# Rounding turns in PSUM with TensorE products in place of a VectorE instruction, in a four-layer spectral kernel

## The chip, the cores and the metric

The kernel runs as one launch on one core of a Trainium2 chip. The metric is the device time of that launch in microseconds (us), as the median of its runs. A core has five engines that run side by side and wait for one another through semaphores: TensorE (PE, matrix products into PSUM), VectorE (DVE), ScalarE (ACT), GpSimd (POOL) and SyncE (SP, which here issues the transfers). Each of them takes its own instructions in order.

## The reference, cut to what matters

An input x of 2048 x 512 passes through four layers, each added to x after a layer norm: A, B, A, B. A is a product with fixed weights in the two-dimensional Fourier domain. B is a convolution along the 2048 positions, one filter K per channel, made through a Fourier transform of twice the length. The filter comes from 128 complex modes per channel, and its making is what the change touches:

```python
dt = jnp.exp(log_dt)
A = -jnp.exp(log_A_real) + 1j * A_imag
C = (C_real + 1j * C_imag) * dt[:, None]
P = jnp.exp((A * dt[:, None])[:, :, None] * pos[None, None, :])
K = 2.0 * jnp.einsum("dn,dnl->dl", C, P).real
```

So for each channel d, position l and mode n the kernel needs a magnitude exp(...) and the sine and cosine of an angle. The angle is counted in turns (one turn is 2 pi). Whole turns change nothing, and the sine instruction is given an angle between minus half a turn and half a turn, so whole turns are taken off first.

## The kernel before, in words

**Stages.** The work of 2048 positions is split as 16 x 128. The first layer A has three parts: `spread` (layer norm and the first Fourier step), `middle` (line 566: `forward`, `weigh`, `back`) and `end` (`fold`, `rows_back`). Layer B works by blocks of 128 channels: `kernel_freq` (line 928) transforms the filter, `forward_norm` and `forward_b` (line 640) the input, `layer_b` (line 970) weighs the two (`weigh`) and transforms back (`back`). Then come the second A and the second B, with the filter's transform kept in memory (kf) from the first time.

**The filter from modes** is `kernel_time` (line 815). Its first inputs come from `kernel_parts` (line 726), which makes, from the raw mode parameters, five rows of values per channel and mode, and splits each into three bf16 parts, which go through memory (parts) into the tile `th` (96 partitions: two halves of three parts of 16 channels). There are 32 units i of 16 channels, and for each unit:

- `grow(i)` (line 834): two products of `th` with constant tiles RM and RP (slices of the constant tile `kb`) into a PSUM tile `pk` and two exponentials by ScalarE into `mag` (line 832 is the helper that records ScalarE's instructions); GpSimd makes a third magnitude (lines 847 and 848).
- for j = 0 and 1, `bend(i, j)` (line 855): four TensorE products of `th` with 256 columns of KQ and KP, also slices of `kb`, put 2 x 256 angles in turns into a PSUM tile `pk` of 128 x 512. VectorE (line 864) adds and takes off a large constant, MAGIC = 1.5 x 2^23, at which float32 has no digits behind the point, and so leaves the rounded turns in the bf16 tile `kw`. TensorE then takes them off the angles in place, as a product of `kw` with `ni`, a negative identity, accumulated onto the same PSUM tile.
- `sine(i, j)` and `cosine(i, j)` (ScalarE, line 832): the absolute angle into the tile `kf`, the sine in place in `pk`, the cosine from `kf` into `qp`.
- `terms(i, j)` (VectorE, lines 886 and 888): four products of sines and cosines with magnitudes into `qp`.
- `total(i, j)`: sixteen TensorE instructions (line 899) sum over the modes into the PSUM tile `pv`; ScalarE copies them to `stage` (line 907), and SyncE writes them to memory (kt).

That makes 64 bends. The helper `halves` (line 330) issues every product as two, on 64 of the 128 weight columns each; the two write to different halves of the PSUM tile's partitions. A float32 product appears in the profile as two instructions, a bf16 product as one.

**What sets the order.** The filter's steps K are not a stage of their own: they are interleaved with layer A's middle and end, and with the first B, by the fractions FILL (lines 1146 to 1217). The final order of each engine's instructions is written out by hand: TURNS (line 1230) holds, for tensor, vector, scalar, gpsimd and sync, a permutation of that engine's instructions as the program issued them, and `take_turns` (line 1500) imposes it. ROOMS (line 1464) gives, for tiles with several buffers, which buffer each use gets. WARM (line 1452) gives places at which `ps` puts products with the tile `warm` ahead of real work: fill, whose results nobody reads. Each of its entries is a number of calls of `halves` with 128 float32 columns, hence four instructions a call. The sum of its entries is 231.

**Buffers.** PSUM has eight banks of 128 x 512 float32. In this part of the kernel three are for `pk`, one for `pv` (PK and PV) and four for layer A or B. The context manager `phase` opens a pool of tiles; a tile got its place there when it was first asked for.

Of the kernel before, what the change touches and what calls it, by code (L numbers as in the profile page):

```python
# [10 lines left out]
F32 = mybir.dt.float32  # L11
# [27 lines left out]
WT = 4  # L39
# [52 lines left out]
def constants():  # L92
# [111 lines left out]
    out["ni"] = -np.eye(128)  # L204
    out["kb"] = kb.reshape(96, 2560)
# [47 lines left out]
class Net:  # L253
# [553 lines left out]
    def kernel_constants(self):  # L807

        BF = mybir.dt.bfloat16
        self.kb = self.sb("kb", [2560], dt=BF, rows=96)  # L810
        self.ni = self.sb("ni", [128], dt=BF)
        self.nc.gpsimd.dma_start(self.kb, self.cst["kb"])
        self.nc.gpsimd.dma_start(self.ni, self.cst["ni"])

    def kernel_time(self, parts, kt, units, group):
# [6 lines left out]
        KQ, RM, RN, KP, RP = (KB[:, k:k + 512] for k in range(0, 2560, 512))  # L822
# [8 lines left out]
        def ordered(*a, **k):  # L831
            nc.scalar.activation(*a, **k)  # L832
# [22 lines left out]
        def bend(i, j):  # L855
# [8 lines left out]
            nc.vector.tensor_scalar(whole, p, MAGIC, -MAGIC, op0=ALU.add, op1=ALU.add)  # L864
            self.halves(p, self.ni, whole, start=False, stop=True, skip_group_check=True)
            live[i, j] = p, mag

        def sine(i, j):
# [3 lines left out]
            ordered(p, p, ACT.Sin, scale=-TAU)  # L872
# [251 lines left out]
def net_kernel(ctx, tc, x, w, ends, kin, log_dt, d_skip, out, **cst):  # L1124
# [19 lines left out]
    with ExitStack() as outer:  # L1144
        with ExitStack() as early:
            early.enter_context(net.phase("pk", P, pk=(2048, PK), pv=(2048, PV)))
            with net.phase("p", P, p1=(2048, 8 - PK - PV), p2="p1", p3="p1"), \
                    net.phase("a", x=(32768, 1), ta=(8192, 1), ca=(6912, 1), u=(16384, 2), w=(2056, WA), wt=(2056, WT),
                              wv="w", junk="w"):
                A = net.layer_a(w, src=xv, dst=hd)  # L1150
                early.enter_context(net.phase("k0", side="right", kb=(5120, 1), ni=(256, 1), th=(1536, TH)))
                net.kernel_constants()
                with net.phase("v", val=(10240, 1), hp=(HP, 2)):
# [5 lines left out]
                    early.enter_context(net.phase("k", side="right", kw=(1024, 2), mag=(6144, MAG),  # L1159
# [10 lines left out]
            outer.enter_context(net.phase("b", t2=(8192, 1), u=(16384, 2), kk=(2048, 8), ta="t2", wt="w", wb="w", xw="w"))  # L1170
# [61 lines left out]
0-17 23-24 18-19 25-28 20-21 32-39 22 29-31 40-65 67-70 76-79 66 80-81 71-72 82-83 73-75 85-88 94-95 84 89-92  # L1232
103-106 93 96-97 112-113 107-108 98-101 109-110 102 114-115 111 116-119 121-124 120 125-126 130-131 127-128
132-133 129 134-161 172-179 163-168 180-181 169-171 182-193 162 194-211 218-219 234-235 212-217 220-221 236-241
222-225 242-249 256-259 226-231 260 264-266 250 267 251 261 232 268-272 252 262 273 253 263 233 274-279 298-307
280-281 254 312 282 286 255 313 287 314 288 315 289 283-285 308-311 316-321 290-291 322-331 338-339 292-295
340-342 346-349 343-345 296-297 350-351 332-335 366-371 358-365 336-337 374-387 414-417 372-373 402-413 418-423
464-465 424-427 388-393 448-451 466-467 452-455 476-483 512-513 456-461 514-515 394-397 516-517 398-401 462-463
428-431 518-519 432-433 520-523 434 436-437 435 438-439 352-357 548-551 554-557 524-525 468-475 552-553 440-441
484-487 558 492-494 504 495 559 505-507 488-491 442-447 496-497 526-533 498-499 508-511 500-503 534-543 560-561  # L1240
544-547 562-564 568 580 569 581 570 582 571 583 565-567 606-609 572-573 586-593 574-577 584 594 578 612 579 595
613 585 610 596-597 611 614-617 620-621 618-619 598-599 626-627 600-601 622-623 628 634-635 629-630 636-637
631-633 654-657 602-605 638-639 660-667 624-625 640-643 658 668-670 688 671 689 659 690-691 646-651 672-673
652-653 644-645 674-677 694-701 678 702-704 692 705 693 679 738-741 706-711 680-685 752-757 712 760 758 761 759
713 742-743 686 762-763 687 764-771 798-800 808-809 801-807 810-811 772-773 812 834-837 813-815 714-721 774-775
784-785 816-819 838-839 786-787 722-729 788-791 840-843 792-795 730-737 844-845 796-797 820-823 826-831 854-857
878 900-902 832-833 744-749 858-863 750-751 910 824-825 846-849 776-777 850-851 778-783 942 903 852-853 904-906
879-880 886-887 864-875 888 881-884 907-908 943-944 894-896 889-890 945 876-877 946-948 885 909 897 911-912
891-893 926-936 949 898 937-938 913-914 939 915-917 899 970-973 940-941 918-925 974-975 962-969 950-961 976-983
986-987 1032-1033 988-989 984-985 990-997 1006-1009 1034-1035 1010-1015 1054-1055 998-1003 1036-1039 1004-1005  # L1250
1056-1057 1076-1077 1040-1043 1016-1023 1044-1045 1066-1067 1024-1031 1078-1081 1068-1075 1046-1051 1082-1083
1052-1053 1084-1089 1094-1097 1092-1093 1090-1091 1058-1063 1110-1113 1100-1101 1132-1135 1098-1099 1102-1109
1116-1123 1130-1131 1114-1115 1136-1137 1064-1065 1138-1139 1164-1169 1140-1143 1146-1147 1124-1127 1148-1149
1144-1145 1150-1151 1128-1129 1152-1153 1184-1187 1154-1155 1202-1205 1156-1163 1170-1171 1188-1189 1172-1181
1206-1207 1182-1183 1190-1193 1296-1299 1208-1209 1194-1201 1314-1329 1268-1275 1330-1331 1300-1313 1332-1333
1210 1212 1214 1217 1211 1213 1219 1221 1215 1223 1225 1216 1218 1227 1220 1222 1224 1226 1388-1395 1228-1230
1232 1231 1233-1234 1236 1235 1237-1238 1240 1239 1241-1242 1244 1243 1245 1470-1477 1454-1461 1246-1252 1254
1253 1255 1257 1256 1258-1259 1261 1260 1262-1263 1265 1264 1267 1266 1478-1483 1494-1497 1462-1469 1276-1280
1282 1281 1283 1285 1284 1286-1287 1289 1288 1290-1291 1293 1292 1295 1294 1484-1487 1506-1509 1488-1489
1510-1517 1490-1493 1518-1521 1530-1533 1498-1505 1536-1539 1548-1553 1534-1535 1372 1370-1371 1373 1375 1374  # L1260
1376 1378 1380 1377 1379 1382 1381 1383-1384 1386 1385 1387 1540-1541 1554-1555 1334-1351 1580 1352-1353
1581-1583 1626-1633 1354-1357 1584-1585 1594-1597 1680-1685 1658-1659 1686-1687 1660-1661 1358-1360 1598-1599
1396-1397 1399 1398 1401 1403 1400 1402 1405 1407 1404 1406 1409 1411 1408 1410 1361-1363 1688-1691 1662-1663
1364-1369 1692-1693 1412-1425 1427 1429 1426 1428 1431 1433 1430 1432 1435 1437 1434 1436 1708-1713 1698-1701
# [283 lines left out]
```

## Time and profile before

| | |
|---|---|
| time, median of 3 runs | 717.33 us |
| lowest and highest run | 716.2 and 723.59 us |
| span of the profiled execution, first to last instruction | 713.4 us |
| instructions profiled | 23503 |
| mean granted TensorE clock | 0.973 |
| bytes moved by DMA, mean rate | 81.32 MB, 114 GB/s |
| first and last rounding by VectorE (line 864) | 79.8 and 382.9 us |

The profiled execution's own time is not listed apart from the three runs; its span lies 3.9 us under their median. Times in the profile count from its first instruction. How to read its lines:

- A row of the windows view gives a stretch in us, its length, then for each engine the busy time and, in brackets, the number of instructions; then the granted TensorE clock (1.00 is full speed), the DMA share and GB/s. Where a view is asked for one tile alone, only the instructions that read or write it count, and engines without any are left out.
- A row of the groups gives line, engine, operation, tiles (output<-inputs), shapes and the count; then busy time in us and the mean duration of one in ns; then how long the engine stood idle ahead of these instructions, and what ended it.
- A row of the waits names who waited for whom, the total in us, the number of times and the longest.
- A row of the timeline gives start, length, engine, line, operation, tiles, shape and how many are merged in it. Products are pipelined, so a length contains a latency; the distance between starts tells how long the array is held.

PEld is the loading of weights, which overlaps products.

### The profile page before, as it was taken

Reading aid. Unit: us, or ns where it says so; the run is one execution under the profiler, and the core shown is the slowest. Engines: PE = TensorE matmul, PEld = TensorE weight load, DVE = VectorE, ACT = ScalarE, POOL = GpSimd, SP = SyncE. Lnnn points to the kernel's source line nnn. Section 1 sums busy time; section 2 is a strip of 40 time slices with the busy share of each in tenths; the row PEclk is TensorE's granted clock in tenths of the full one; section 3 lists DMA queues with packets and bytes.
Section 4 is the critical chain, followed back from the end, with each engine's and each line's share of the span. In section 5 each row is a group of like instructions: output and inputs, shape, how many; then the busy total and the mean of one; then the engine's idle time right before and its main releaser. Section 6 shows DMA issues by size and latency. Waiting matters only on the chain. (4 is left out here: it accounts for less than half of the span.)

```text
span 713.4 us, 23503 instructions
## 1 busy us (share of the span) xinstructions
PE 626.0 (88%) x9580; PEld 491.3 (69%) x9580; DVE 601.9 (84%) x1348; ACT 438.2 (61%) x946; POOL 357.3 (50%) x565
## 2 busy tenths in 40 slices
PE   4459989989996999889999997984989899999996
PEld 3237867878674867667858876774877766577876
DVE  4998497998999799969999676869588699799993
ACT  3558999997664796778868524333767427333322
POOL 1533528672852704543196356452056484286870
PEclk9779999999999999999999999997999999999999
DMA  8602611613558350455544689222123103335514
GB/s 282 229 0 89 210 48 47 122 62 43 167 133 245 107 138 32 65 128 94 163 62 136 195 198 246 80 106 75 61 77 89 46 2 104 125 103 149 156 34 111
DMA packets 137355, 81.32 MB, mean 114 GB/s; under 512 B 70976, under 2 KB 116928, under 8 KB 136352
## 3 DMA queue, kind: packets, MB, share of 16 engines
q1 hardware_dynamic: 136992, 79.30, 40.1%
q8 instruction: 76, 1.25, 0.7%
q0 software_dynamic: 256, 0.52, 0.4%
q14 instruction: 31, 0.25, 0.1%
HBM read 54.90 MB, written 25.43 MB: 113 GB/s over the span
## 5 line engine op out<-in xcount | busy, mean ns | idle before, releaser
L1003 POOL TENSOR_TENSOR u<-wb,wb 64x512 f32<-64x512 f32 x90 | 123.2, 1373 | 66.0 <-DVE wb L991 60.9
L336 PE MATMUL p<-z,mb 128*64 128x512 f32 (+2 forms) x480 | 108.0, 517 | 1.7 <-DVE wb L991 1.3
L899 PE MATMUL pv<-qp 128*64 128x128 f32 x1024 | 81.6, 279 | 5.0 <-ACT stage L907 4.2
L991 DVE TENSOR_TENSOR wb<-p,kk 128x512 f32<-128x512 f32 x128 | 81.5, 676 | 4.3 <-POOL u L1003 2.3
L336 PEld LDWEIGHTS p<-mb,u 128*64 128x64 f32 x2048 | 73.1, 138 | 13.1 <-issue 6.7
L336 PE MATMUL p<-mb,u 128*64 128x64 f32 x2048 | 74.3, 223 | 4.4 <-issue 2.0
L663 ACT COPY z<-p 128x512 f32<-128x512 f32 x96 | 52.4, 595 | 41.8 <-PE p L336 31.6
L669 DVE STREAM_TRANSPOSE z<-z 128x512 f32<-128x512 f32 x96 | 59.3, 675 | 19.8 <-ACT z L663 19.7
L899 PEld LDWEIGHTS pv<-qp 128*64 128x64 f32 x1024 | 64.4, 139 | 15.8 <-ACT stage L907 6.9
L1113 POOL TENSOR_SCALAR w<-w,norms 128x128 f32<-128x128 f32 x64 | 34.7, 554 | 67.7 <-DMA w<-h 29.8
L547 POOL TENSOR_TENSOR w<-w,w 64x257 f32<-64x257 f32 x48 | 34.7, 724 | 66.8 <-DVE w L542 45.3
L1015 ACT COPY u<-p 128x512 f32<-128x512 f32 x64 | 35.9, 590 | 48.7 <-PE p L336 45.3
L330 PE MATMUL p<-w,w 128*64 128x256 f32 x256 | 38.2, 438 | 27.8 <-DVE w L463 11.6
L330 PE MATMUL pk<-kb,th 96*64 96x256 bf16 (+1 forms) x384 | 56.5, 312 | 1.5 <-DVE qp L888 1.1
L542 DVE TENSOR_TENSOR w<-wt,p 128x514 f32<-128x514 f32 x64 | 42.7, 688 | 17.1 <-PE p L336 9.6
L864 DVE TENSOR_SCALAR kw<-pk 128x512 bf16<-128x512 f32 x64 | 42.9, 680 | 16.5 <-PE pk L330 16.1
L330 PE MATMUL p<-warm 128*64 128x128 f32 x612 | 49.2, 284 | 3.2 <-DVE half L1139 1.1
L336 PE MATMUL p<-t,w 64*64 64x128 f32 x1024 | 42.1, 280 | 10.2 <-DMA w<-kt 3.5
L336 PEld LDWEIGHTS p<-z,mb 128*64 128x64 f32 x480 | 39.7, 137 | 16.1 <-issue 7.9
L330 PEld LDWEIGHTS p<-w,w 128*64 128x64 f32 x256 | 24.7, 156 | 36.3 <-DVE w L463 12.7
L336 PE MATMUL p<-w,ca 128*64 128x257 f32 x256 | 45.0, 385 | 4.1 <-ACT w L526 1.5
L832 ACT ACTIVATE kf<-pk 128x512 f32<-128x512 f32 x64 | 38.8, 606 | 15.4 <-PE pk L330 13.8
(179 smaller groups left out, 1617.1 us busy)
## 6 DMA issues: line engine op xcount, KB each, us to landing
wt<-in_w SPq DMA_DIRECT2D x32, 257.0 KB, 2.7
kf<-kk SPq DMA_DIRECT2D x32, 256.0 KB, 3.3
kk<-kf SPq DMA_DIRECT2D x32, 256.0 KB, 2.7
u<-in_x SPq DMA_DIRECT2D x16, 256.0 KB, 6.8
hr<-in_x SPq DMA_DIRECT2D x16, 256.0 KB, 3.9
kt<-stage SPq DMA_DIRECT2D x32, 128.0 KB, 5.2
h<-hr SPq DMA_DIRECT2D x16, 256.0 KB, 3.0
w<-kt SPq DMA_DIRECT2D x32, 128.0 KB, 3.1
```

The costliest lines, as they stand in the source:

```text
L330: self.nc.tensor.matmul(out[64 * r:64 * r + 64], weights[:, 64 * r:64 * r + 64], data, **k)
L336: last = self.nc.tensor.matmul(out, weights, data, start=not more, stop=True, skip_group_check=True).ins
L542: nc.vector.tensor_mul(m[pl], W, px[:, None, :].to_broadcast([128, 2, 257]))
L547: e[0].tensor_sub(Y[0:64, v], m[0][hs, 0], m[1][hs, 1])
L663: nc.scalar.copy(tiles["z"][:, :, :, b, m:m + 2].rearrange("p u j m r -> p (u j) (m r)"), ps[b].rearrange("p u j m r -> p (u j) (m r)"))
L669: nc.vector.transpose(tiles["zt"][:, u:u + 8].rearrange("p u j d -> p (u j d)"), tiles["z"][:, u:u + 8].rearrange("p u j b m r -> p (u j b ...
L832: nc.scalar.activation(*a, **k)
L864: nc.vector.tensor_scalar(whole, p, MAGIC, -MAGIC, op0=ALU.add, op1=ALU.add)
L899: nc.tensor.matmul(p[64 * t:64 * t + 64, g], QP[:, c, 2, d:d + 2].rearrange("p s a -> p (s a)"), QP[:, c, 0:2, d:d + 2].rearrange("p k s b ...
L991: nc.vector.tensor_mul(split(m[c, pl], "du", [32, 16]), by_channel(p), split(k[c], "du", [32, 16]))
L1003: self.added = e[0].tensor_sub(y[0:64], v[0, 0], v[1, 1]), e[1].tensor_add(y[64:128], v[0, 1], v[1, 0])
L1015: nc.scalar.copy(V[:, :, j, :, d:d + 8].rearrange("p n q d -> p q n d"), p.rearrange("p (q n) d -> p q n d", q=2))
```

## The change

`bend` no longer uses VectorE. TensorE adds MAGIC to the angles in PSUM, as a product whose weights are a row of ones (`ni`, now 256 columns: a first row of 1 in the first half, of -1 in the second, zero elsewhere) and whose data is a tile `big` full of MAGIC; a second product takes MAGIC off. What stays in PSUM is the rounded turns. Then the angles themselves are taken off by four more products of `th` with LQ and LP, which are KQ and KP with the sign turned. What is left is the rounded turns less the angle, where it was the angle less the rounded turns, so the sine's scale changes its sign. The tile `kw` goes, `kb` grows from 2560 to 3584 columns, and a GpSimd memset fills `big`.

Beside it, `phase` reserves a place for every buffer when it opens, in the order in which its tags are written, and two of the phases list their tags in another order. TURNS is rewritten for all five engines, and ROOMS for nearly all tiles. WARM has other places, and the sum of its entries is 145.

```diff
@@ constants
-    out["ni"] = -np.eye(128)
-    out["kb"] = kb.reshape(96, 2560)
+    first = np.zeros((128, 2, 128))
+    first[0, 0], first[0, 1] = 1, -1
+    out["ni"] = first.reshape(128, 256)
+    out["kb"] = np.concatenate([kb, -kb[:, :, :512], -kb[:, :, 1536:2048]], 2).reshape(96, 3584)
@@ phase
             for tag, v in tags.items():
                 self.tags[tag] = self.tags[v] if isinstance(v, str) else (pool, name, tag, *v)
+            for tag, v in tags.items():
+                if not isinstance(v, str):
+                    for k in range(v[1]):
+                        room = f"{tag}{k}" if v[1] > 1 else tag
+                        pool.tile([128, v[0] // 4], F32, tag=room, bufs=1, name=f"{name}_{room}")
             yield
@@ kernel_constants
-        self.kb = self.sb("kb", [2560], dt=BF, rows=96)
-        self.ni = self.sb("ni", [128], dt=BF)
+        self.kb = self.sb("kb", [3584], dt=BF, rows=96)
+        self.ni = self.sb("ni", [256], dt=BF)
+        self.big = self.sb("big", [512], dt=BF)
+        self.nc.gpsimd.memset(self.big, MAGIC)
@@ kernel_time
-        KQ, RM, RN, KP, RP = (KB[:, k:k + 512] for k in range(0, 2560, 512))
+        KQ, RM, RN, KP, RP, LQ, LP = (KB[:, k:k + 512] for k in range(0, 3584, 512))
@@ bend
-            whole = self.sb("kw", [512], dt=BF)
             p = self.ps("pk", [2, 256])
-            self.halves(p[:, 0], th[:, h, 0], KQ[:, e], start=True, stop=False, skip_group_check=True)
-            self.halves(p[:, 1], th[:, h, 1], KP[:, e], start=False, stop=False, skip_group_check=True)
+            a, b = th[:, h, 0], th[:, h, 1]
+            self.halves(p[:, 0], a, KQ[:, e], start=True, stop=False)
+            self.halves(p[:, 1], b, KP[:, e], start=False, stop=False)
+            p0, p1 = p[:, 0], p[:, 1]
             p = p.rearrange("p k d -> p (k d)")
-            nc.vector.tensor_scalar(whole, p, MAGIC, -MAGIC, op0=ALU.add, op1=ALU.add)
-            self.halves(p, self.ni, whole, start=False, stop=True, skip_group_check=True)
+            self.halves(p, self.ni[:, 0:128], self.big, start=False, stop=False)
+            self.halves(p, self.ni[:, 128:256], self.big, start=False, stop=False)
+            self.halves(p0, a, LQ[:, e], start=False, stop=False)
+            self.halves(p1, b, LP[:, e], start=False, stop=True)
             live[i, j] = p, mag
@@ sine
-            ordered(p, p, ACT.Sin, scale=-TAU)
+            ordered(p, p, ACT.Sin, scale=TAU)
@@ net_kernel
-                    net.phase("a", x=(32768, 1), ta=(8192, 1), ca=(6912, 1), u=(16384, 2), w=(2056, WA), wt=(2056, WT),
+                    net.phase("a", x=(32768, 1), u=(16384, 2), ta=(8192, 1), w=(2056, WA), ca=(6912, 1), wt=(2056, WT),
...
-                early.enter_context(net.phase("k0", side="right", kb=(5120, 1), ni=(256, 1), th=(1536, TH)))
+                early.enter_context(net.phase("k0", side="right", kb=(7168, 1), ni=(512, 1), big=(1024, 1), th=(1536, TH)))
...
-                    early.enter_context(net.phase("k", side="right", kw=(1024, 2), mag=(6144, MAG),
+                    early.enter_context(net.phase("k", side="right", mag=(6144, MAG), 
...
-            outer.enter_context(net.phase("b", t2=(8192, 1), u=(16384, 2), kk=(2048, 8), ta="t2", wt="w", wb="w", xw="w"))
+            outer.enter_context(net.phase("b", kk=(2048, 8), t2=(8192, 1), u=(16384, 2), ta="t2", wt="w", wb="w", xw="w"))
@@ WARM: 92 entries, sum 231, become 98 entries, sum 145
-WARM = {22: 7, 35: 3, 55: 1, 104: 3, 116: 2, 120: 5, 123: 6, 146: 2, 158: 1, 160: 2,
...
+WARM = {39: 7, 56: 2, 62: 1, 77: 1, 86: 1, 163: 3, 481: 1, 484: 1, 524: 1, 527: 1, 542: 1, 564: 1,
...
```

More of the change, by code (lines that the diff above doesn't have):

```diff
@@ L1237 @@
[L1237 to L1251, printed above, removed]
@@ new lines @@
+559-561""",
+    "sync": """
+0-1 4-6 2 7 27 9-11 14 13 34 16 8 12 17 15 19 18 38 20 105 30 3 35 31 21-24 26 25 28 32 109 33 36 29 37 41 40
+106 42 68 70 74 39 72 44 83 45 50 43 51-52 86 66 48 46 53 49 55 77 47 57 54 64 58 63 56 65 60 62 61 59 76 85 69
+67 71 94 73 88 100 90 75 92 78 84 79-82 91 96 128 102 87 93 98 134 97 99 101 89 95 108 107 104 110 112 111 115
+114 125 124 113 131 130 129 132 103 126-127 137 140 147 122 120 123 116 133 117 135 118 136 121 143-145 139 138
+146 119 154 184 141 159 142 167 149 148 160-161 174 169 171 163 158 153 155 157 151 150 175 156 164-165 168 166
```

447 lines of the change are left out of this document (219 added, 228 removed), and 21 rows, old and new, of tables (TURNS, WARM).

## The prediction, made before the changed kernel was run

> **What bounds the kernel now.** First the page's busy times, then the engines by stretch: before the filter's steps begin, the stretch that holds them, and the rest.
>
> ```profile
> PE 626.0 (88%) x9580; PEld 491.3 (69%) x9580; DVE 601.9 (84%) x1348; ACT 438.2 (61%) x946; POOL 357.3 (50%) x565
> ```
>
> ```profile
> core 0: us, PE busy (x) PEld busy (x) DVE busy (x) ACT busy (x) POOL busy (x), PEclk, DMA share, GB/s
> 60.00:400.00 340.00, 315.21 (x4663) 249.00 (x4660) 303.96 (x667) 270.88 (x553) 173.58 (x301) 0.99 0.43 111
> 0.00:60.00 60.00, 30.73 (x218) 21.06 (x220) 49.60 (x133) 30.20 (x67) 21.60 (x45) 0.83 0.47 155
> 400.00:714.00 314.00, 280.10 (x4707) 221.21 (x4702) 248.33 (x549) 137.08 (x328) 162.10 (x220) 0.98 0.38 109
> ```
>
> TensorE and VectorE look equally full, but an average hides which of them sets the pace. All 64 roundings lie between 60 and 400 us, so I cut that stretch where its character changes:
>
> ```profile
> 60.00:80.00 20.00, 20.00 (x241) 17.81 (x236) 10.06 (x20) 18.75 (x40) 7.40 (x20) 1.00 0.48 148
> 80.00:160.00 80.00, 73.42 (x1027) 60.88 (x1026) 72.08 (x129) 75.66 (x172) 50.16 (x115) 1.00 0.33 90
> 160.00:180.00 20.00, 18.22 (x262) 15.81 (x260) 17.18 (x36) 16.05 (x34) 6.33 (x11) 1.00 0.31 43
> 180.00:240.00 60.00, 54.14 (x694) 38.59 (x692) 59.80 (x176) 34.73 (x69) 35.72 (x62) 0.97 0.65 191
> 240.00:260.00 20.00, 19.35 (x283) 14.64 (x278) 15.08 (x42) 16.92 (x33) 7.62 (x14) 1.00 0.38 72
> 260.00:300.00 40.00, 37.62 (x538) 27.23 (x538) 39.34 (x85) 31.71 (x60) 18.81 (x19) 1.00 0.30 71
> 300.00:340.00 40.00, 35.73 (x640) 29.93 (x638) 31.91 (x62) 32.40 (x64) 14.56 (x23) 0.96 0.49 108
> 340.00:400.00 60.00, 56.74 (x1002) 44.12 (x1000) 58.50 (x123) 44.67 (x86) 32.98 (x39) 1.00 0.43 112
> ```
>
> VectorE is never free in 180 to 240, 260 to 300 and 340 to 400: it is idle 0.20 + 0.66 + 1.50 = 2.4 us in 160. There it is the bound. In 80 to 160 ScalarE is the fuller (idle 4.3 us of 80, VectorE 7.9). In 160 to 180, 240 to 260 and 300 to 340 no engine is full in earnest, for much of what TensorE does is fill (products on the warm tile, whose results nobody reads):
>
> ```profile
> 60.00:400.00 340.00, 49.12 (x620) 37.28 (x620) 0.00 (x0) 0.99 0.43 111
> ...
> 180.00:240.00 60.00, 8.03 (x108) 6.11 (x108) 0.00 (x0) 0.97 0.65 191
> ...
> 260.00:300.00 40.00, 11.43 (x150) 8.59 (x152) 0.00 (x0) 1.00 0.30 71
> ...
> 340.00:400.00 60.00, 5.98 (x84) 4.82 (x84) 0.00 (x0) 1.00 0.43 112
> ```
>
> These are the fill's rows alone (PE, PEld, DVE). Without fill TensorE is busy 266 of 340 us, VectorE 304, ScalarE 271.
>
> **What is removed.** One VectorE instruction per bend. The groups by line give its price, and by stretch (columns PE and DVE) the instructions that write or read its tile are:
>
> ```profile
> L864 DVE TENSOR_SCALAR kw<-pk 128x512 bf16<-128x512 f32 x64 | 42.9, 680 | 16.5 <-PE pk L330 16.1 <-PE p L336 0.2
> ```
>
> ```profile
> 80.00:160.00 80.00, 8.70 (x32) 11.21 (x17) 1.00 0.33 90
> 160.00:180.00 20.00, 4.38 (x16) 4.71 (x7) 1.00 0.31 43
> 180.00:240.00 60.00, 2.79 (x16) 5.35 (x8) 0.97 0.65 191
> 240.00:260.00 20.00, 2.05 (x10) 3.33 (x5) 1.00 0.38 72
> 260.00:300.00 40.00, 3.52 (x18) 6.03 (x9) 1.00 0.30 71
> 300.00:340.00 40.00, 3.85 (x18) 5.46 (x8) 0.96 0.49 108
> 340.00:400.00 60.00, 4.05 (x20) 6.62 (x10) 1.00 0.43 112
> ```
>
> In the three VectorE stretches it takes 5.35 + 6.03 + 6.62 = 18.0 us, and nothing there covers it: **-18.0** (ends: -18.0, and 0 if another engine takes over at once). In 80 to 160 it takes 11.2 us, but ScalarE has only 4.3 us to give: **-1** (ends 0 and -4.3), the lower side because little of ScalarE's idling there waits for the rounding. In the three mixed stretches it takes 4.71 + 3.33 + 5.46 = 13.5 us. There the round trip itself also costs:
>
> ```profile
> DVE kw L864 <- PE pk L330: 6.5, 1, 6.5
> ```
>
> ```profile
> ACT kf L832 <- PE pk L330: 13.8, 12, 2.8
> ```
>
> The first is VectorE's longest wait in 300 to 340, standing at the head of its queue for the turns it is to round, with everything behind it. The second is ScalarE over 60 to 400, waiting for the product that takes the rounded turns off. Both waits lose a link: after the change ScalarE follows TensorE directly. I take half of the 13.5: **-7** (ends 0 and -13.5).
>
> **What is added.** Six more TensorE instructions per bend: two pairs over 256 columns, LQ and LP, and one pair more over 512, for the constant is put on and taken off (two pairs) where the rounded turns were taken off (one). The two halves of a pair run side by side, so I price pairs by the distance of starts in the timeline:
>
> ```profile
> 99.91 0.41 PE L330 MATMUL pk<-kw,ni 128*64 128x512 bf16 x2
> 100.12 0.63 PE L330 MATMUL pv<-warm 128*64 128x128 f32 x8
> 100.56 0.71 PE L899 MATMUL pv<-qp 128*64 128x128 f32 x9
> ```
>
> ```profile
> 158.70 0.39 PE L330 MATMUL pk<-kb,th 96*64 96x256 bf16 x4
> 158.92 0.72 PE L899 MATMUL pv<-qp 128*64 128x128 f32 x10
> ```
>
> A 512-column pair holds the array for 100.12 - 99.91 = 0.21 us, two 256-column pairs for 158.92 - 158.70 = 0.22 us, and two fill calls (eight instructions) for 100.56 - 100.12 = 0.44 us. A bend thus grows from 0.22 + 0.21 = 0.43 to 2 x 0.22 + 2 x 0.21 = 0.86 us: 64 x 0.43 = **27.5 us** of array time more. Against it the list of fill calls falls from 231 to 145 in the diff: 86 x 0.22 = 18.9 us less. Net 8.6 us. In the three VectorE stretches lie 27 bends, 11.6 us, and TensorE is not busy there for 5.9 + 2.4 + 3.3 = 11.6 us and is in fill for another 25.4: hidden. In 80 to 160 lie 17 bends, 7.3 us, against 6.6 us not busy beside the fill: hidden. What is not hidden is a product for which another engine waits and which now stands behind twelve in TensorE's queue in place of six. I take **+5**, a little over half of the net, between 0 and 27.5.
>
> **Smaller edits.** The pk bank is free sooner, since nothing waits between its first product and ScalarE's read: no price of its own, it is how the gains above come about. The constant load, now 3584 columns in place of 2560, and the memset of the constant's tile stand on POOL's queue at the start:
>
> ```profile
> L330 PE MATMUL pk<-kb,th x384: 269/274/634, 70.7 to 379.8; 96*64 96x256 bf16 x128, 96*64 96x512 bf16 x64
> L812 POOL DMA_DIRECT2D kb<-in_kb x1: 732/732/732, 1.3 to 1.3; - x1
> ...
> DMA to landing us min/median/max: 8.6/8.6/8.6
> ```
>
> Issued at 1.3 us, it lands 8.6 us later, 12 us if it grows with its columns, and the first use is at 70.7: 0. The cover is layer A's own start; without it the 12 us would be paid once. The kw tiles go; ScalarE's sine only changes the sign of its scale: 0. The rooms are now reserved when a phase opens, in a written order, and the orders of all queues, SP's and POOL's too, are rewritten: the trace has no row for that. Its bound is taken from VectorE's idle time in the stretch that the edit itself does not touch, 60.0 - 49.6 = 10.4 us before 60: I take 0, with 10 us either way.
>
> **Sum.** -18.0 - 1 - 7 + 5 = -21 us on a span of 713.4: 692.4. The shown runs' median is 717.33, 3.9 us above the span, so the time is **696.3**, written 696.
>
> **A rule of the Trainium skill.** The third table has TensorE busy 93% of 60 to 400 by matmuls and 249 of 340 us, 73%, by weight loads. The Trainium skill, "Perfetto Trace Analysis", section "Identifying the Most-Contended Engine", says that matmul busy time misjudges this engine's headroom and that weight-load busy time is to be used. By it the array has some 27% left, the 27.5 us fit, and the +5 becomes 0: 691. By the matmul row it is nearly full, which is the first rival below. The fill's 49 us in that row bear the rule out in part.
>
> **Rivals.** (1) **TensorE becomes the bound; slower.** Place: 60 to 400, its in-order queue. If the 93% shown (315.2 of 340) is its ceiling and the fill that remains is needed, its work is 266.1 + 27.5 + the fill cut by 86 x 0.22 = 30.2, in all 323.8, and the stretch takes 323.8 / 0.927 = 349 us: +9, so 726. It decides from the point at which the stretch's work passes 315 us, so if the fill falls by less than 27.5 us. For it: 20.00 of 20 in 60 to 80. Against: without its fill it is free for 74 us of the stretch. (2) **ScalarE takes over; no change.** It is busy 270.9 of 340 us and keeps every Abs, Sin and Exp; when VectorE falls to 304 - 43 = 261, ScalarE is the fullest. If VectorE's freed time is then mostly spent waiting for it, the 26 us of the three gains shrink to about 5 and the +5 stands: 717. For it: 80 to 160. Against: 25 us of idle ScalarE in 180 to 240. (3) **All of it comes through.** 42.9 us and the 6.5 us wait, with the products hidden: 713.4 - 42.9 - 6.5 + 3.9 = 668, and 6.9 us above that, since in 80 to 160 ScalarE can give only 4.3 of the 11.2: 675. (4) **The clock falls.** Even with fill there are stretches below full clock:
>
> ```profile
> 220.00:240.00 20.00, 16.52 (x270) 13.56 (x268) 19.87 (x82) 10.00 (x19) 5.82 (x9) 0.91 0.81 247
> ```
>
> That is 0.09 x 20 = 1.8 us of clock lost once. Five more such dips, with 86 fill calls gone, cost 9 us: 705. The Trainium skill, "TensorE: Matmul & The Clock Gate", section on the clock gate, has the clock halved after an idle window of about 3.4 us; this row agrees: 1.8 us lost is 3.6 us at half clock. Against it: twelve products per bend keep the array busy by themselves.
>
> **Chances.** Forecast, 682 to 710: 0.50. Rival 3: 0.10. Rival 4: 0.07. Rival 2: 0.16. Rival 1: 0.17. A measurement here tells about 1% from no change. Faster by over 1%: 0.50 + 0.10 + 0.07 = 0.67; within 1%: 0.16; slower: 0.17. The range runs from rival 3 to rival 1, 675 to 726; the forecast's own is 682 to 710.
>
> **What would show it.** Right: no kw rows; 256 products on the constant and 512 over 256 columns on the kb tile; VectorE's busy time near 559 us, at most 262 in the filter's stretch; that stretch ending near 380; fill near 145 calls, which at four instructions each are 580; ScalarE's wait before kf below 13.8 us. The forecast is wrong if the filter's stretch ends no earlier although VectorE has 43 us less to do: then look at whether ScalarE (rival 2) or TensorE without fill (rival 1) is the one without gaps. It is also wrong in its reasons if the gain lies after 400 us, where the edit removes nothing, or if the granted clock falls in places that had fill.

## The result: 735.9 us, slower by 2.9%, all of it after 609 us

The changed kernel's median is 735.91 us (734.37 to 738.49) against 717.33: a ratio of 1.029, interval 1.025 to 1.033. The prediction was 696, with 675 to 726 as its range. The page of the changed kernel, the line of busy times (engine, us, share of the span, instructions):

```profile
PE 674.6 (92%) x9620; PEld 497.8 (68%) x9620; DVE 574.5 (78%) x1284; ACT 437.6 (60%) x944; POOL 358.5 (49%) x566
```

VectorE is busy 27 us less (the roundings took 42.9, what is left takes longer than before), TensorE 49 us more, and the share that weight loads take hardly moves. To find where the time went I look for milestones first: the last `kf` of the filter (first and last start of the eleven or ten in the window), and the last rows of the layer norm ahead of the second layer B. The changed kernel:

```profile
L841 ACT ACTIVATE kf<-pk x10: 597/602/606, 340.9 to 385.2; 128x512 f32<-128x512 f32 x10
```

```profile
607.79 1.52 ACT L634 ACTIVATE x<-za,lnn 128x512 f32<-128x512 f32 x2
```

The kernel before:

```profile
L832 ACT ACTIVATE kf<-pk x11: 593/597/623, 340.7 to 390.1; 128x512 f32<-128x512 f32 x11
```

```profile
608.95 0.82 ACT L627 ACTIVATE x<-za,lnn 128x512 f32<-128x512 f32 x1
```

The filter is 5 us ahead at its end, and at 609 us both kernels stand at the same place. So the whole difference of the spans, 732.6 - 713.4 = 19.2 us, lies in the last stage (second layer B), which the edit does not touch. That is the difference to the kernel before; against the forecast of 696 the gain that was expected ahead of 609 us is missing too. The windows, changed kernel first (PE, PEld, DVE, ACT, POOL, clock):

```profile
60.00:400.00 340.00, 332.03 (x4594) 247.89 (x4598) 272.87 (x600) 270.74 (x548) 171.69 (x295) 1.00 0.44 112
400.00:609.00 209.00, 191.33 (x2744) 145.48 (x2736) 165.51 (x404) 102.40 (x259) 102.29 (x178) 0.98 0.38 106
609.00:733.00 124.00, 117.84 (x2034) 83.13 (x2032) 85.95 (x139) 33.92 (x67) 60.83 (x45) 0.97 0.32 94
```

```profile
400.00:609.00 209.00, 184.42 (x2793) 146.00 (x2790) 161.92 (x410) 103.23 (x262) 100.57 (x175) 0.98 0.39 110
609.00:714.00 105.00, 95.68 (x1918) 75.21 (x1914) 86.40 (x139) 33.84 (x68) 61.52 (x45) 0.99 0.37 108
```

In the last stage every engine is about as busy as before except TensorE, which is busy 22 us longer. There products of `t` and `x` are copied to the tile `z` by ScalarE and transposed by VectorE, and the 512-column products of `z` and `mb` follow. The shape behind the names (`128*64`, `64*64`) is the part of the array that an instruction uses; the kernel puts two of the first kind, or four of the second, side by side. The groups there, changed kernel and then before (busy us, mean ns of one):

```profile
L343 PE MATMUL p<-z,mb 128*64 128x512 f32 x96 | 41.7, 615 | 0.0
L337 PE MATMUL p<-warm 128*64 128x128 f32 x164 | 23.0, 289 | 0.7 <-ACT z L670 0.7
L343 PE MATMUL p<-t,x 64*64 64x128 f32 x398 | 21.4, 294 | 0.3 <-ACT x L634 0.3
```

```profile
L336 PE MATMUL p<-z,mb 128*64 128x512 f32 x96 | 33.4, 601 | 0.3 <-DVE z L669 0.3
L336 PE MATMUL p<-t,x 64*64 64x128 f32 x414 | 16.7, 276 | 0.2 <-ACT z L663 0.2
L330 PE MATMUL p<-warm 128*64 128x128 f32 x32 | 3.0, 282 | 0.0
```

Two things are to be seen. There is more fill (x164 in place of x32), and the same 96 wide instructions on `z` hold TensorE 8.3 us longer though one of them takes nearly as long as before. So it is their overlap that is lost. (The rows overlap one another, so their growths do not add up to the 22 us.) The timeline shows how (start, length); changed kernel, then before:

```profile
655.41 0.45 PE L343 MATMUL p<-t,x 64*64 64x128 f32 x8
655.79 1.97 PE L343 MATMUL p<-u,t 128*64 128x128 f32 x32
657.69 0.45 PE L343 MATMUL p<-t,x 64*64 64x128 f32 x8
658.07 1.07 PE L343 MATMUL p<-z,mb 128*64 128x512 f32 x2
659.07 0.45 PE L343 MATMUL p<-t,x 64*64 64x128 f32 x8
659.45 0.64 PE L343 MATMUL p<-z,mb 128*64 128x512 f32 x1
```

```profile
645.36 1.08 PE L336 MATMUL p<-z,mb 128*64 128x512 f32 x4
646.37 1.10 PE L336 MATMUL p<-t,x 64*64 64x128 f32 x32
647.41 2.84 PE L336 MATMUL p<-u,t 128*64 128x128 f32 x48
```

Before, both halves of a wide product (x4, a float32 product being two instructions) hold TensorE for 646.37 - 645.36 = 1.01 us. In the changed order one half stands alone between 64x64 products, and that half (x2) takes 659.07 - 658.07 = 1.00 us: as long as the pair, with half of the array empty. And eight 64x64 instructions by themselves take 655.79 - 655.41 = 0.38 us, while 32 in a row take 1.04, 0.26 for eight: each short visit to that shape costs 0.12 us more than its share of a long one. The Trainium skill, "TensorEngine Tiling (Array Packing)", section "Tiling Modes", says under its key properties that a change of tiling mode drains TensorE and that tiles of one mode work in parallel; both rows agree.

The order as written out by hand can be counted for this. In the last stage 21 of 36 groups of 512-column products have something between their parts (4 before), and changes of tile shape went from 37 to 71; ahead of it from 54 to 162. Who waits for it is in the waits of the last stage, changed kernel and before (us in total, times, longest):

```profile
ACT z L670 <- PE p L343: 38.8, 12, 6.9
POOL u L1015 <- DVE wb L1003: 35.1, 9, 19.0
...
DVE wb L1003 <- PE p L343: 16.5, 13, 2.7
```

```profile
ACT z L663 <- PE p L336: 13.3, 10, 2.7
```

ScalarE's wait for the products that fill `z` grows from 13.3 to 38.8 us, VectorE waits for the products on `z` behind it, and GpSimd for VectorE: all of them for TensorE in the end. The clock is a small part at most: 0.97 over 124 us and 0.99 over 105 make 3.7 and 1.1 us lost, 2.7 us apart.

### The profile page after: what moved, and what is told of

It is laid out like the page before. It is cut to its first block, busy times and chain, and to the rows that moved or that the text cites. A ratio compares the mean times of both kernels' runs of the same rounds, so it can differ in the third digit from the quotient of the medians.

```text
span 732.6 us, 23416 instructions
## 1 busy us (share of the span) xinstructions
PE 674.6 (92%) x9620; PEld 497.8 (68%) x9620; DVE 574.5 (78%) x1284; ACT 437.6 (60%) x944; POOL 358.5 (49%) x566
## 5 line engine op out<-in xcount | busy, mean ns | idle before, releaser
L343 PE MATMUL p<-z,mb 128*64 128x512 f32 (+2 forms) x480 | 141.6, 524 | 0.8 <-DVE wb L1003 0.7
L911 PE MATMUL pv<-qp 128*64 128x128 f32 x1024 | 97.5, 277 | 1.4 <-ACT stage L919 1.3
L337 PE MATMUL pk<-kb,th 96*64 96x256 bf16 (+1 forms) x640 | 89.0, 297 | 2.9 <-ACT mag L841 1.6
L337 PEld LDWEIGHTS p<-warm 128*64 128x64 f32 x528 | 46.7, 144 | 34.3 <-issue 23.2
L337 PE MATMUL p<-warm 128*64 128x128 f32 x528 | 64.4, 289 | 5.4 <-ACT x L482 4.4
L343 PEld LDWEIGHTS p<-mb,u 128*64 128x64 f32 x2048 | 66.4, 138 | 2.1 <-issue 2.0
L676 DVE STREAM_TRANSPOSE z<-z 128x512 f32<-128x512 f32 x96 | 59.0, 676 | 10.9 <-ACT z L670 10.4
L549 DVE TENSOR_TENSOR w<-wt,p 128x514 f32<-128x514 f32 x64 | 42.4, 687 | 23.9 <-PE p L343 14.3
L337 PEld LDWEIGHTS <-th 96*64 96x64 bf16 x640 | 47.6, 109 | 18.8 <-issue 10.1
L343 PE MATMUL p<-t,w 64*64 64x128 f32 x1024 | 54.3, 283 | 1.9 <-DMA t<-in_t 0.8
L337 PE MATMUL p<-ca,u 128*64 128x128 f32 (+2 forms) x512 | 55.6, 301 | 0.3 <-ACT u L570 0.3
L343 PEld LDWEIGHTS p<-t,w 64*64 64x64 f32 x1024 | 34.2, 132 | 27.6 <-issue 21.8
```

The costliest lines, as they stand in the source:

```text
L337: self.nc.tensor.matmul(out[64 * r:64 * r + 64], weights[:, 64 * r:64 * r + 64], data, **k)
L343: last = self.nc.tensor.matmul(out, weights, data, start=not more, stop=True, skip_group_check=True).ins
L549: nc.vector.tensor_mul(m[pl], W, px[:, None, :].to_broadcast([128, 2, 257]))
L676: nc.vector.transpose(tiles["zt"][:, u:u + 8].rearrange("p u j d -> p (u j d)"), tiles["z"][:, u:u + 8].rearrange("p u j b m r -> p (u j b ...
L911: nc.tensor.matmul(p[64 * t:64 * t + 64, g], QP[:, c, 2, d:d + 2].rearrange("p s a -> p (s a)"), QP[:, c, 0:2, d:d + 2].rearrange("p k s b ...
```

## The experiments

Theory 1: the new order of TensorE's queue carries the loss, because it sets apart calls that would fill the array together, changes tile shape more often and has more fill in the last stage. By 1a in the expectations it is mostly the setting apart and the shapes, by 1b the fill. The rivals are the edit's own products, and the other engines' orders. Theory 2 came with the second set: TensorE also sets the end of the filter's stretch, where the edit's products and the fill stand in its way. The kernel before was run beside each set, with medians of 717.8 (the first four), 716.1 (the second four), 716.8 (the third four) and 718.7 (the last three). Ratios are against those; differences in us between runs of different sets are uncertain by the 2.6 us that these medians spread.

### Edit and order taken apart

**The edit alone**, under the orders, rooms and fill of before. The bend's diff is that of the change; in TensorE's order each bend's last pair becomes eight products at its place.

```diff
-            whole = self.sb("kw", [512], dt=BF)
...
-            nc.vector.tensor_scalar(whole, p, MAGIC, -MAGIC, op0=ALU.add, op1=ALU.add)
-            self.halves(p, self.ni, whole, start=False, stop=True, skip_group_check=True)
+            self.halves(p, self.ni[:, 0:128], self.big, start=False, stop=False)
+            self.halves(p, self.ni[:, 128:256], self.big, start=False, stop=False)
+            self.halves(p0, a, LQ[:, e], start=False, stop=False)
+            self.halves(p1, b, LP[:, e], start=False, stop=True)
```

> The rounding in PSUM under the orders, buffers and fill of before: eight products stand where the last pair of a batch stood, and VectorE's 64 roundings are gone. Theory 1 (the new orders carry the loss, and the edit itself is worth something in the filter's stretch): at most 717, and 696 if the prediction's terms for the edit hold. Rival (the added products are the loss: TensorE is the bound wherever they run): the 27.5 us of added array time that the prediction took as its upper bound show, 735 to 745.

Measured: 742.3, ratio 1.034 (1.028 to 1.039). So what theory 1 expected of the edit itself fell: under the old order it is no gain but costs 24.5 us net, close to the 27.5 that its products were priced at, and no gain from VectorE's 43 us shows. The waits of TensorE between 60 and 600 us name one part of it:

```profile
PE p L338 <- DMA w<-kt: 14.1, 8, 6.2
```

The first B's products on the filter (`w` from `kt`) are reached in TensorE's queue while the filter they need is late (3.5 us of such waits before). I read it as an order made for one pace of the filter that does not fit another; no run tests that by itself.

**The last stages exchanged.** The changed kernel with all orders, rooms and fill of the last stage from before, and the reverse. Of the fill, for instance:

```diff
-        1509: 3, 1521: 1, 1525: 1, 1532: 1, 1535: 1, 1540: 7, 1547: 1, 1551: 1, 1560: 1, 1579: 1,
...
+        1509: 3, 1522: 2, 1524: 3, 1525: 2, 1526: 2, 1528: 2, 1532: 2, 1535: 1, 1548: 3}
```

> The changed kernel, with all engines' orders, the buffers' turns and the fill of the last stage (second layer B, which the edit doesn't touch) taken from before. Theory 1 (the loss is in this stage's own new order): its span from the last first-norm result at 609 us to the end goes from 124 back to about 104 us, total 714 to 718. Rival (the edit, or what it leaves behind at 609 us, slows the last stage): 730 to 736, as the changed kernel.

> The kernel before, with the last stage's orders, buffers' turns and fill taken from the changed kernel; no product of the edit is in it. Theory 1: the last stage costs 124 in place of 104 us, total 733 to 738. Rival (the edit, not the order): no change, 716 to 719.

Measured: 718.2, ratio 1.003 (0.999 to 1.006), and 741.7, ratio 1.033 (1.028 to 1.038). The second lies above the 733 to 738 that theory 1 gave. The loss moves with the last stage's orders, rooms and fill, in a kernel with the edit and in one without it. The wide products' row moves with it too; first the changed kernel with the old last stage, then the kernel before with the new one:

```profile
L343 PE MATMUL p<-z,mb 128*64 128x512 f32 x96 | 33.4, 601 | 0.3 <-DVE z L676 0.3
```

```profile
L336 PE MATMUL p<-z,mb 128*64 128x512 f32 x96 | 41.6, 613 | 0.0
```

### What in the last stage's order

**Gathering.** From here on "gathered" means: in TensorE's order, calls that fill the array together (the two 64-column halves of a product, the four 64x64 blocks of a group) stand next to one another; other engines' orders stay. In the changed kernel's last stage the first places are:

```diff
-4152-4155 4180-4195 4156 4196-4197 4164-4165 4157-4163 4198-4203 4166-4167 4204-4213
+4152-4155 4180-4197 4156-4157 4164-4165 4158-4163 4198-4205 4166-4167 4206-4213
```

> The changed kernel with one thing moved in the last stage: in TensorE's order the calls that fill the array together (the two 64-column halves of a product, the four 64x64 blocks of a group) stand behind one another again, at the place of the first. Fill and the other engines' orders stay. Theory 1a (calls set apart and changes of tile shape are what the new order costs): 715 to 722. Rival 1b (the fill, or the other engines' orders, carry it): 729 or more.

Then only the 128-row products, so that 4156 and 4157 join but 4196 and 4197 stay behind them, and only the 64x64 groups:

```diff
-4180-4195 4156 4196-4197
+4180-4195 4156-4157 4196-4197
```

> The changed kernel; in the last stage only the 128-row calls are gathered: 21 of 36 groups of 512-column products stood apart (4 of 36 before), none does now; the 64x64 groups stay as they are (12 of 64 apart). If products running alone with half of the array empty are the last stage's loss: 10 to 14 us come off, 722 to 726. If changes of tile shape are (they only go from 71 to 63): 733 or more.

```diff
-4180-4195 4156 4196-4197
+4180-4197 4156
```

> The changed kernel; in the last stage only the 64x64 groups are gathered (13 of 64 apart, none now), the wide ones stay apart. Changes of tile shape go from 71 to 61; at 0.14 us for one, as the rows of the last stage show, that is 1 to 2 us, with the shares of the array that the blocks leave empty 4 at most: 731 to 735. If the changes of shape carry the loss instead, 722 to 728.

And the fill of the last stage left out (all entries of WARM from 1521 on), with its order kept:

```diff
-        1509: 3, 1521: 1, 1525: 1, 1532: 1, 1535: 1, 1540: 7, 1547: 1, 1551: 1, 1560: 1, 1579: 1,
...
+        1509: 3}
```

> The changed kernel without the 43 fill calls of the last stage (86 calls of halves; before has 22), its other order kept. Theory 1a (calls set apart and changes of shape carry most of the last stage's loss): at most 6 us come back, 729 to 736. Rival 1b (the fill carries it, 23 us of it are in this stage's rows): 714 to 724.

| changed kernel, in its last stage | us | against 735.9 | ratio to before |
|---|---|---|---|
| gathered | 722.8 | -13.1 | 1.006 (1.003 to 1.009) |
| only 128-row products gathered | 726.8 | -9.1 | 1.012 (1.006 to 1.018) |
| only 64x64 groups gathered | 732.0 | -3.9 | 1.020 (1.013 to 1.027) |
| fill left out | 730.3 | -5.6 | 1.017 (1.012 to 1.022) |
| all of it as before | 718.2 | -17.7 | 1.003 (0.999 to 1.006) |

The two gatherings add up to the whole one, 9.1 + 3.9 = 13.0, and with the fill to 18.7 of 17.7 us, though no run has gathering and no fill together. The whole gathering and the wide products alone end just above what theory 1a gave them (722.8 against 715 to 722, 726.8 against 722 to 726); the other two lie inside. So setting apart, with the changes of shape that it brings, carries the larger part, and the fill the smaller one. The groups' rows say that each edit did its own part. All gathered:

```profile
L343 PE MATMUL p<-z,mb 128*64 128x512 f32 x96 | 33.4, 600 | 0.0
L343 PE MATMUL p<-t,x 64*64 64x128 f32 x396 | 18.1, 298 | 0.0
L337 PE MATMUL p<-warm 128*64 128x128 f32 x164 | 16.6, 285 | 1.4 <-ACT z L670 1.4
```

Only the 128-row products:

```profile
L343 PE MATMUL p<-z,mb 128*64 128x512 f32 x96 | 33.4, 603 | 0.0
L343 PE MATMUL p<-t,x 64*64 64x128 f32 x406 | 21.3, 300 | 0.0
```

Only the 64x64 groups:

```profile
L343 PE MATMUL p<-z,mb 128*64 128x512 f32 x96 | 42.1, 620 | 0.0
...
L343 PE MATMUL p<-t,x 64*64 64x128 f32 x396 | 18.7, 300 | 0.0
```

The row on `z` is 33.4 or 42 by whether the halves are neighbours, and the row on `t` 18 or 21 by whether the blocks are.

### What bounds the filter's stretch

**Fill left out there.** Places of WARM that stand between the filter's first and last product are emptied, in the kernel before, in the edit alone, and in the mixed kernel of 718 (the changed one with the old last stage). For the kernel before, for instance:

```diff
-WARM = {22: 7, 35: 3, 55: 1, 104: 3, 116: 2, 120: 5, 123: 6, 146: 2, 158: 1, 160: 2,
...
+WARM = {22: 7, 35: 3, 55: 1, 104: 3, 1105: 7, 1108: 1,
```

> The kernel before without those 152 fill calls and with nothing else changed. If VectorE bounds the filter's stretch there, as the prediction has it, the fill is hidden: 712 to 720, or slower where the granted clock falls. If TensorE bounds it before as well: 33 us at most come off, 684 to 705.

> The edit under the orders of before, and the 152 fill calls that stand between the filter's first and last product are left out (304 calls of halves; they compute nothing). Theory 2 (in the filter's stretch the edit's products and the fill both stand in TensorE's way, and the change could afford the edit there because it had thinned the fill from 152 calls to 30): 25 to 33 us come back of the 742, 709 to 717. Rival (what the edit adds is a wait between engines, not array time, so the fill was hidden; or the granted clock falls without it): 735 or more.

> The changed kernel with the last stage of before, and without the 30 fill calls left in the filter's stretch. Theory 2: 4 to 7 us come off 718, 711 to 714. Rival (another engine ends that stretch, or the clock falls): 717 or more.

Measured: 710.7, ratio 0.989 (0.984 to 0.995); 731.9, ratio 1.020 (1.015 to 1.025); 713.3, ratio 0.996 (0.992 to 0.999). The 152 calls, 33 us of array time, are worth 5.4 us in the kernel before, 10.4 under the edit alone. The first lies between its two expectations, nearer to the one with VectorE as the bound; the second missed both, at 731.9 between 717 and 735. The third, 713.3, is as theory 2 had it. So theory 2 holds in part, and I take it that neither engine bounds that stretch alone: with TensorE relieved by 33 us, VectorE is busy 306 of 340 us, where it was 304 (kernel before without fill):

```profile
60.00:400.00 340.00, 297.97 (x4068) 218.53 (x4065) 306.35 (x674) 270.93 (x554) 171.98 (x302) 0.97 0.44 112
```

The clock there is 0.97 in place of 0.99, and the time is shorter all the same.

**The rounding products twice, and left out,** in the mixed kernel of 718:

```diff
             self.halves(p, self.ni[:, 0:128], self.big, start=False, stop=False)
             self.halves(p, self.ni[:, 128:256], self.big, start=False, stop=False)
+            self.halves(p, self.ni[:, 0:128], self.big, start=False, stop=False)
+            self.halves(p, self.ni[:, 128:256], self.big, start=False, stop=False)
```

```diff
-            self.halves(p, self.ni[:, 0:128], self.big, start=False, stop=False)
-            self.halves(p, self.ni[:, 128:256], self.big, start=False, stop=False)
```

> The mixed kernel of 718 (the changed kernel with the last stage of before), with the constant added and taken off a second time: 256 more 512-column products behind the first 256, the sums unchanged by them. In the last stage's rows two halves of a product of this kind take 0.21 us as the prediction priced them, 27 us in all. Theory 2 (TensorE's array sets the end of the filter's stretch): 20 to 30 us come on, 738 to 748. If the prediction's sum holds (most of such work is hidden there): 0 to 12 us, 718 to 730.

> The mixed kernel of 718 without the products that add and take off the constant: 256 products of 512 columns fewer, and the turns aren't rounded. Theory 2: 20 to 27 us come off, 691 to 698. Rival (VectorE or ScalarE stands right behind TensorE and ends the stretch): 708 or more.

The second leaves the turns unrounded. Measured: 736.1, ratio 1.025 (1.022 to 1.029), and 711.0, ratio 0.992 (0.989 to 0.996). So 27 us more for TensorE cost 18, just under theory 2's range (738 to 748) and above the other (718 to 730), and 27 us less give 7, as the rival had it. Added work comes through for two thirds, saved work for a quarter, which fits TensorE as the bound with another limit close behind it. That limit need not be an engine: without these products the clock between 60 and 400 us is 0.97, in the mixed kernel 0.99, which is 0.02 x 340 = 6.8 us of TensorE's time.

### Gathered everywhere

The changed kernel with its own fill, last stage and other orders, gathered before the last stage too where the waits allow it (1500 of 5258 places of TensorE's order change):

```diff
-302-303 298 314-317 304-307 260-261 308-309 262-263 299 318-329
+302-303 298-299 314-317 304-307 260-261 308-309 262-263 318-329
```

> The changed kernel with its own last stage, its own fill and all its other orders; only TensorE's calls that fill the array together stand next to one another, before the last stage and in it. Theory 1 (setting them apart is the loss of the new order): the 13 us of the last stage come back and some 12 to 18 before it, 705 to 712, so the changed kernel would be faster than the one before. Rival (the gain of the gathered mixed kernel came from the fill left out or from the last stage of before): 718 to 724.

And two without the filter's fill: the mixed kernel gathered, and, without the edit, the kernel before gathered.

> The mixed kernel without the filter's fill (713), and with TensorE's calls that fill the array together put next to one another before the last stage too, wherever the waits allow it: changes of tile shape go from 200 to 158 and groups set apart from 248 to 72 of 2375. Theory 1 (this is what the new order loses, in the filter's stretch as in the last stage): 15 to 30 us come off, 683 to 698. Rival (that stretch has its end from other engines by now): 708 to 714.

> The kernel before without the filter's fill (711) and with the same gathering: groups set apart go from 246 to 2 of 2295, changes of shape from 92 to 82, but few of those set apart are wide products. Theory 1: at most 6 us come off, 704 to 711. If the edit is worth anything once both orders are treated alike, the gathered kernel with the edit ends before this one; if its products cost more than VectorE's roundings did, this one ends first.

Measured: 700.9, ratio 0.976 (0.971 to 0.982); 694.7, ratio 0.969 (0.964 to 0.974); 709.8, ratio 0.989 (0.986 to 0.993). Gathering alone takes 35.0 us off the changed kernel, more than the 24 to 31 expected, and makes it faster than the one before; the two others came out as theory 1 had them. Without the filter's fill, gathering takes 18.6 us off the mixed kernel (713.3 to 694.7) and only 0.9 off the kernel before (710.7 to 709.8): the loss belongs to the new order. So the gathered kernel with the edit is 15.0 us faster than the one without. That pair differs in more than the edit: the first also has the orders and rooms that were written for it, so the 15 us belong to the edit and these together. The edit under the gathered order of before was not run. The second, 694.7, is the fastest of all here and beats both kernels.

These groups have the same products in the same number, in another order; the page's groups for three kernels, before, changed, changed and gathered:

```profile
L336 PE MATMUL p<-z,mb 128*64 128x512 f32 (+2 forms) x480 | 108.0, 517 | 1.7 <-DVE wb L991 1.3
L899 PE MATMUL pv<-qp 128*64 128x128 f32 x1024 | 81.6, 279 | 5.0 <-ACT stage L907 4.2
...
L336 PE MATMUL p<-t,w 64*64 64x128 f32 x1024 | 42.1, 280 | 10.2 <-DMA w<-kt 3.5
```

```profile
L343 PE MATMUL p<-z,mb 128*64 128x512 f32 (+2 forms) x480 | 141.6, 524 | 0.8 <-DVE wb L1003 0.7
L911 PE MATMUL pv<-qp 128*64 128x128 f32 x1024 | 97.5, 277 | 1.4 <-ACT stage L919 1.3
...
L343 PE MATMUL p<-t,w 64*64 64x128 f32 x1024 | 54.3, 283 | 1.9 <-DMA t<-in_t 0.8
```

```profile
L343 PE MATMUL p<-z,mb 128*64 128x512 f32 (+2 forms) x480 | 110.8, 526 | 1.5 <-DVE wb L1003 0.7
L911 PE MATMUL pv<-qp 128*64 128x128 f32 x1024 | 85.5, 276 | 1.7 <-ACT stage L919 1.4
...
L343 PE MATMUL p<-t,w 64*64 64x128 f32 x1024 | 44.8, 282 | 3.6 <-DMA w<-kt 1.5
```

The mean of one never moves (517 to 526, 276 to 279, 280 to 283 ns); the busy time of the group does: it rises by 34, 16 and 12 us, and 31, 12 and 10 of these come back. A group's busy time over its count times its mean says how far its members overlap, and here only the order was changed between the last two. The filter's end in the gathered kernel:

```profile
L841 ACT ACTIVATE kf<-pk x8: 597/600/607, 341.6 to 369.1; 128x512 f32<-128x512 f32 x8
```

## Why the prediction was wrong

**The step that failed** is the last of the smaller edits: "the orders of all queues, SP's and POOL's too, are rewritten: the trace has no row for that [...] I take 0, with 10 us either way". Its bound came from VectorE's idle time ahead of 60 us, while the cost lay in TensorE's queue. The last stage's new orders and fill cost 17.7 us (exchanged into the changed kernel) to 23.9 (exchanged into the one before), and what gathering returns over the whole kernel is 35.0: 13.1 in the last stage and some 22 ahead of it. The miss of 40 us has the same two parts: 17.7 us in the last stage, and ahead of it the whole forecast gain, since with the last stage of before the kernel stands at 718.2. Groups set apart and changes of shape could have been counted in the diff without a run. Their price was only half on hand: the trace of before had calls that stand together (a pair of halves in 1.01 us, eight 64x64 instructions in 0.26), while the half alone in 1.00 us and the eight alone in 0.38 are rows of the changed kernel.

**"The two halves of a pair run side by side"** was right of the new products, which stand together in either order, but was taken as a property of the helper. In these traces it holds for calls that are neighbours in the order.

**The +5 for TensorE** failed too, in its cover: the products were to hide in VectorE's stretches, in fill and in time not busy. Under the old order the edit costs 24.5 us net, without the filter's fill still 731.9 - 710.7 = 21.2. That fill was little room kept free: 33 us of it were worth 5.4, and 10.4 under the edit.

**The fill was counted as a total** (231 to 145 calls), not by place. In the filter's stretch it fell from 152 calls to 30, and in the last stage it rose from 8 (32 instructions, above) to 41. The fill's own rows, changed kernel:

```profile
60.00:400.00 340.00, 17.46 (x120) 12.72 (x120) 0.00 (x0) 1.00 0.44 112
609.00:733.00 124.00, 23.00 (x164) 15.63 (x164) 0.00 (x0) 0.97 0.32 94
```

The thinner fill, the new orders and the rooms ahead of 609 us together paid for the edit (742.3 to 718.2; not taken apart), the last stage was then lost on top (718.2 to 735.9).

**VectorE's 18 + 7 us.** VectorE's work in the stretch fell from 304 to 272.9 us, not to 262, and the filter ended 5 us earlier, not 10. The roundings are gone in full, but other rows of VectorE grew by some 11 us over the kernel (the 64 products of `qp` and `mag` over 512 columns from 44.2 to 48.2); why is open. The forecast named this case ("if the filter's stretch ends no earlier although VectorE has 43 us less to do") and named the engine to look at: TensorE, busy 332.0 of 340. Under an order that lets TensorE keep up, the last `kf` starts at 369.1 in place of 390.1, and the edit with the orders written for it is worth 15 us between two gathered kernels. So a gain from the edit is there, smaller than forecast, but it needed a TensorE order that the change did not bring; under the orders of before the edit alone lost.

**The rivals.** TensorE as the bound (726) was the right engine with the wrong place and price: it reckoned the stretch from 60 to 400 by instructions. By these the stretch would hold 315.2 + 27.5 - 31.7 (the fill's row, 49.1 to 17.5) = 311 us of TensorE; it holds 332, and the loss came from overlap that was lost there and in the last stage. ScalarE did not take over (its wait for the filter's turns fell from 13.8 to 7.0 us). The clock did not fall where the fill went: 1.00 from 60 to 400. The dip that the prediction set beside an idle window of 3.4 us does not bear that length out: in the kernel before, the clock was 0.63 from 230 to 232 us and 0.52 from 232 to 234, so the 3.6 us are the time at half clock, while TensorE had stood idle for 2.39 us ahead of it.

**The rule on weight loads** misled as it was used here, as room for added work. The Trainium skill, "Perfetto Trace Analysis", section "Identifying the Most-Contended Engine", judges TensorE's headroom by its share of the peak rate and by weight-load busy time. In the last stage the share of weight loads fell from 75.21 of 105 us to 83.13 of 124, 72% to 67%, while TensorE's matmul busy time rose from 91% to 95% and the other engines came to wait for it. That fits an array that stands half empty in part: the room was there, and gathering took 13.1 us of it, but in the order as written other work could not use it.

**Open.** How much of the 24.5 us of the edit alone is array time and how much the waits of an order that no longer fits was not separated. Nor was the loss ahead of the last stage (some 22 us by gathering) split into halves apart and changes of shape, as it was for the last stage. Of the last stage's 17.7 us, what the other engines' orders and the rooms did was not run by itself.

## What to carry to other kernels

When a change rewrites an engine's order, price the order: count in it the calls that share the array and no longer stand together, and the changes of tile shape, stage by stage, before pricing the edit itself. Count by kind: all groups set apart are about as many in the kernel before and in the mixed one (246 and 248, both without the filter's fill), but of the 96 groups of products on `z` in the whole kernel 21 stand apart in the order of before and 64 in the changed one. A group whose busy time grows while the mean of one instruction stays the same has lost overlap, not speed. And before calling an engine free because others look full or because part of its work is fill, ask what a known amount of added work does to the end: here 27 us more cost 18, and 27 us less gave 7.

## What the runs showed of the hardware

Half of a wide float32 product, alone between 64x64 products, held TensorE as long as both halves together (1.00 and 1.01 us). Eight 64x64 instructions by themselves held it 0.12 us longer than eight out of a run of 32 (0.38 and 0.26). And the granted clock stayed at 1.00 between 60 and 400 us with 17 us of fill in place of 49, where TensorE was busy for 332 of 340 us.
